# Attention logits from two fp32r parts on alternating row halves of the array, instead of three bf16 parts

## The chip, the cores and the metric

The kernel runs on one core of a Trainium2 chip. The metric is the device time of one execution in microseconds (us); lower is better.

## The reference

Two independent computations on inputs of 2048 x 576 each, joined along the last axis.

```python
# A: memory-augmented attention, 32 heads of 18, 4 segments of 512 rows
q,k,v = x@wq, x@wk, x@wv                 # split into heads and segments
for s in range(4):
    logits = qs @ ks.T * 18**-0.5 + mask # mask: -1e9 above the diagonal
    p = softmax(logits)
    a_dot = p @ vs
    a_mem = (phi(qs) @ M) / (phi(qs) @ z + 1e-6)
    o = g*a_mem + (1-g)*a_dot            # g = sigmoid(beta) of the head
    M += phi(ks).T @ vs;  z += phi(ks).sum(0)
out_a = concat(o) @ wo
# B: irfft2(rfft2(x) * (w_r + 1j*w_i))
```

Queries and keys come from weights scaled up by 200, so logits are large, and the kernel carries q and k in split precision.

## The kernel before

One program, in this order: forward FFT of B with the first weights of A (0 to about 73 us); projections of A beside the middle of the FFT on VectorE (to about 282 us); inverse FFT beside a prologue of attention (to about 356 us); attention with output projection (to the end). Instructions of each engine run in the order in which the code emits them.

**Projections.** `projections` runs over 4 segments g and 13 units each: nine `qk_unit`s (128 output rows of q and k by 512 columns, 14 fp32r matmuls in `passes`, L461) and four `v_unit`s. The matmuls of several units are in flight in five PSUM banks `pj`, while ScalarE (ACT) and VectorE (DVE) work off the older ones. A `qk_unit` splits its result into three bf16 parts in tile `sp3`: cast (L474), subtract in PSUM (L481), cast (L488), subtract again with a matmul against a negative identity `nid` (L490), cast (L491). SyncE's (SP) queue then writes them to DRAM: `qkD`, and for the two odd dimensions of each head (mt equal to 4) `reD`.

**Stacks.** Heads are worked on in groups n of eight (16 groups, four to a segment). `stack_dmas` reads a group's q or k back as a stack of 108 rows: dimension times part, in the combinations of parts that are needed (48+32+16 rows from `qkD`, 12 from `reD`). One matmul of 108 rows then gives the logits in split precision. Three buffers hold q stacks (`Qs`) and four k stacks (`Ks`). A quad k is half a group: four heads. Rows 108 and 109 hold the row maxima in two bf16 parts against -1 in `Ks`, so that the second pass subtracts them in the matmul.

**First pass, `s1(t)`,** for head t of 128: logits with queries on the partitions, in three PSUM tiles of the three banks `s1`: query blocks 2 and 0 in `pa` (384 and 128 columns, each with a matmul `idb` x `tri` of 128 columns that adds the causal mask, L666), block 3 in `pc` (512), block 1 in `pb` (256). DVE takes the row maxima: one reduction over blocks of 128 for `pa` (L667), one custom mask-and-reduce each for `pc` and `pb` (L661). `mpath(k)` turns a quad's maxima: small DVE, ACT and GpSimd (POOL) operations, a transpose on TensorE (PE), a copy, and a DMA into rows 108 and 109 of `Qs`.

**Second pass, `s2(t)`:** logits with keys on the partitions (L702: 512 columns, L706 and L707: 384 and 128 into one bank, L711: 256), exponentials on ACT (L703, L708, L712), and at a quad's end causal zeroing on POOL (L716). `pv` multiplies with the values in fp32, one 32-column tile of the array for each head of the quad (L731), in two of every four iterations.

**The loop** in `attention` runs t from 0 to 132. Iteration t emits, piece by piece in turn, s1 of head t+11 (generator `a`) and s2 of head t (generator `b`), then `pv` of the quad before; `run_bg` puts in a step of background work (`den`, `mixed`, `oproj`: L785, L804, L810, L851, L874). Up to t=116 both passes run in an iteration. `prologue` does s1 of the first 11 heads beside the inverse FFT, one piece at a time. `last_proj` and what stands around it form the end.

Of the kernel before, what the change touches and what calls it, by code (L numbers as in the profile page):

```python
# [340 lines left out]
BF=mybir.dt.bfloat16  # L341
# [43 lines left out]
class ATT:  # L385
    def __init__(s,nc,tc,io,cp,dp):
        s.nc,s.tc,s.io=nc,tc,io
        s.ident=cp.tile([128,128],F32,name="ident"); s.bm=cp.tile([126,7,19],F32,name="bm")
        s.tri=cp.tile([128,128],BF,name="tri"); s.idb=cp.tile([128,128],BF,name="idb")
# [3 lines left out]
        s.qkD=[d(f"qkD{i}",[8,3,128,512],BF) for i in range(4)]  # L393
        s.reD=[d(f"reD{i}",[24,32,512],BF) for i in range(4)]
# [68 lines left out]
    def qk_unit(s,g,mt,tp,pp):  # L463
# [5 lines left out]
        sp3=tp.tile([128,3,512],BF,name="sp3",bufs=3)  # L469
# [3 lines left out]
        j=[2,1,0] if mt>4 else [0,1,2]  # L473
        nc.scalar.copy(sp3[:,j[0]],ps)  # L474
# [6 lines left out]
        nc.vector.tensor_tensor(ps,ps,sp3[:,j[0]],op=OP.subtract)  # L481
# [6 lines left out]
        nc.scalar.copy(sp3[:,j[1]],ps)  # L488
        yield
        nc.tensor.matmul(ps,s.nid,sp3[:,j[1]],start=False,stop=True,skip_group_check=True)  # L490
        nc.scalar.copy(sp3[:,j[2]],ps)  # L491
        if mt!=4: nc.sync.dma_start(s.qkD[g][mt-(mt>4)].rearrange("i p c -> p i c"),sp3)
        else:
            for r,i,c,n in ((0,0,1,3),(0,1,1,2),(0,2,1,1),(64,0,3,3),(64,0,2,2),(64,0,1,1)):
                m={3:0,2:3,1:5}[n]; a=s.reD[g][r*12//64+2*m]
                x=sp3[r:r+64,i:i+c] if c==n else sp3[r:r+64,i:i+1].to_broadcast([64,n,512])
                nc.sync.dma_start(bass.AP(tensor=a.tensor,offset=a.offset,ap=[[512,64],[64*512,n],[1,512]]),x)
# [48 lines left out]
    def projections(s,xp,tp,pp,wv,pace,hook):  # L546

        live=[]
        s.nid=wv.tile([128,128],BF,name="nid"); s.nc.scalar.activation(s.nid,s.ident,AF.Copy,scale=-1.0)
# [25 lines left out]
    def att_setup(s,cp):  # L575
        nc,io=s.nc,s.io
        s.Qs+=[cp.tile([128,8,512],BF,name=f"Qs{i}") for i in range(1,3)]
        s.Ks+=[cp.tile([128,8,512],BF,name=f"Ks{i}") for i in range(1,4)]
# [10 lines left out]
    def stacks0(s,pool):  # L589

        t=pool.tile([128,9,512],F32,name="x0",tag="x0",bufs=1)
        q,k=[t[:,4*i:4*i+4].rearrange("p a c -> p (a c)").bitcast(BF).rearrange("p (a c) -> p a c",a=8) for i in range(2)]
        s.Qs,s.Ks,s.mask=[q],[k],t[:,8]; s.loaded=set()
        s.nc.sync.dma_start(s.mask,s.io["mask"])
        return s.stack_dmas(0,0)+s.stack_dmas(0,1)
    def masks(s):
        nc=s.nc
        nc.scalar.copy(s.tri,s.mask[:,384:])
        nc.scalar.copy(s.idb,s.ident)
# [553 lines left out]
```

## Time and profile before

| | us |
|---|---|
| runs (3) | 709.8, 709.96, 713.46; median 709.96 |
| the profiled execution | 710.93 |
| its span, first to last instruction | 709.2 |
| TensorE busy | 679.2 (96%) |
| VectorE busy | 551.2 (78%) |
| ScalarE busy | 451.3 (64%) |
| mean granted clock of TensorE | 1.000 |

PE is TensorE's matmuls, PEld its weight loads, which overlap them. A matmul's recorded duration includes a tail that overlaps the next one, so sums of durations say more than the time that passes; the distance from one start to the next is what a matmul costs. "f32" in a matmul row stands for fp32 and fp32r alike. A form such as 108*128 gives the rows and columns of the array in use.

### The profile page before, as it was taken

The page shows a single profiled execution, that of the slowest core. Times are in us where ns is not written, and L with a number is a line of the kernel's source. Part 1 is how long each engine was busy: PE and PEld are TensorE (multiplying, and loading weights), DVE is VectorE, ACT ScalarE, POOL GpSimd, SP SyncE. Part 2 cuts the span into 40 slices and gives each one's busy share as a digit, 9 for nine tenths or more (in the row PEclk, how much of TensorE's full clock was granted, in tenths as well). Part 3 has the DMA queues.
Part 4 walks back from the last instruction along what each step waited for, and adds up shares of the span by engine and source line. Part 5 has one row for each costly group of instructions (what it writes and reads, how often), then busy time and mean ns, then how long its engine had stood idle before and what let it go on. Part 6 is the DMA issues. An engine that isn't in the chain of part 4 may idle for free. (4 is left out here: it accounts for less than half of the span.)

```text
span 709.2 us, 14404 instructions
## 1 busy us (share of the span) xinstructions
PE 679.2 (96%) x4991; PEld 501.4 (71%) x4991; DVE 551.2 (78%) x1262; ACT 451.3 (64%) x986; POOL 209.8 (30%) x403
## 2 busy tenths in 40 slices
PE   4999999999999999999999899999999999999997
PEld 4988869879879879999954454445566445663487
DVE  5999979899799779787787887888657876567533
ACT  3665797485587474544378777777656776567421
POOL 5432000100200102655235333444323652235300
PEclk9999999999999999999999999999999999999999
DMA  8996455576385688899339886886656767442152
GB/s 308 289 286 171 132 159 185 162 208 203 91 234 177 167 209 294 199 253 262 110 111 207 182 175 137 197 202 159 152 131 176 190 159 158 89 127 67 28 156 82
DMA packets 71146, 123.80 MB, mean 175 GB/s; under 512 B 12184, under 2 KB 39174, under 8 KB 67482
## 3 DMA queue, kind: packets, MB, share of 16 engines
q1 hardware_dynamic: 64422, 106.89, 57.3%
q0 software_dynamic: 5632, 15.76, 8.2%
q8 instruction: 39, 0.64, 0.4%
q10 hardware_dynamic: 1020, 0.25, 0.2%
q14 instruction: 33, 0.27, 0.2%
HBM read 82.10 MB, written 39.81 MB: 172 GB/s over the span
## 5 line engine op out<-in xcount | busy, mean ns | idle before, releaser
L661 DVE CUSTOM_DVE_ANT_0 junk<-s,x 128x512 bf16<-128x512 f32 x248 | 137.0, 552 | 57.9 <-PE s L653 53.1
L716 POOL TENSOR_SCALAR_AFFINE_SELECT P<-P 128x512 f32<-128x512 f32 (+2 forms) x132 | 78.4, 625 | 113.6 <-ACT P L703 104.8
L667 DVE TENSOR_REDUCE mx<-s 128x4 f32<-128x512 f32 x128 | 87.7, 685 | 5.2 <-PE s L666 3.3
L703 ACT ACTIVATE P<-s 128x512 f32<-128x512 f32 x128 | 77.7, 607 | 12.6 <-PE s L702 4.6
L731 PE MATMUL pv<-P,vs 128*32 128x512 f32 (+3 forms) x1024 | 82.5, 439 | 0.1
L708 ACT ACTIVATE P<-s 128x512 f32<-128x512 f32 x128 | 77.5, 606 | 2.4 <-PE s L707 2.2
L712 ACT ACTIVATE P<-s 128x256 f32<-128x256 f32 x128 | 49.9, 390 | 44.7 <-PE s L711 44.2
L653 PE MATMUL s<-Ks,Qs 108*128 108x384 bf16 (+3 forms) x256 | 69.1, 301 | 1.5 <-DVE mx L667 1.2
L731 PEld LDWEIGHTS pv<-P,vs 128*32 128x32 f32 x1024 | 26.9, 109 | 45.3 <-issue 34.5
L461 PE MATMUL pj<-x,wqkh 128*128 128x512 f32 x162 | 56.5, 409 | 0.0
L653 PEld LDWEIGHTS <-Qs 108*128 108x128 bf16 x320 | 31.5, 98 | 24.4 <-issue 13.0
L205 DVE TENSOR_TENSOR Z<-t,t 128x290 f32<-128x290 f32 (+1 forms) x96 | 48.4, 555 | 0.1
L519 POOL MEMSET vt<- 128x32 f32 x16 | 2.4, 167 | 149.0 <-PE pm L529 127.7
L205 DVE TENSOR_TENSOR t<-Z 128x580 f32<-128x580 f32 x64 | 46.1, 757 | 0.0
L142 PE MATMUL f<-ftab,eh 128*128 128x290 f32 (+1 forms) x160 | 32.6, 323 | 11.8 <-DMA ftab<-ftab 9.2
L666 PE MATMUL s<-tri,idb 128*128 128x128 bf16 x256 | 43.0, 219 | 0.0
L295 PE MATMUL i<-civ,Y 128*128 128x256 f32 (+1 forms) x288 | 39.3, 289 | 0.2 <-POOL Y L280 0.2
L295 PEld LDWEIGHTS i<-civ,Y 128*128 128x128 f32 (+1 forms) x288 | 36.6, 181 | 1.0 <-POOL Y L280 0.4
L306 PE MATMUL i<-itab,T 128*128 128x290 f32 (+1 forms) x224 | 36.7, 306 | 0.0
L142 PEld LDWEIGHTS f<-ftab,eh 128*128 128x128 f32 (+1 forms) x160 | 26.1, 206 | 14.0 <-issue 8.6
L461 PE MATMUL pj<-x,wqkl 128*128 128x512 f32 x90 | 35.5, 395 | 0.0
L461 PE MATMUL pj<-xh,wqkl 128*128 128x512 f32 x90 | 35.5, 395 | 0.0
(210 smaller groups left out, 1830.2 us busy)
## 6 DMA issues: line engine op xcount, KB each, us to landing
qkD<-sp SPq DMA_DIRECT2D x32, 384.0 KB
xin<-xb SPq DMA_DIRECT2D x16, 384.0 KB
cfw<-cfw POOLq DMA_DIRECT2D x16, 384.0 KB, 4.3
civ<-civ POOLq DMA_DIRECT2D x16, 384.0 KB, 8.8
vs<-vD SPq DMA_DIRECT2D x16, 330.0 KB
vD<-vt SPq DMA_DIRECT2D x16, 311.0 KB
W<-w SPq DMA_DIRECT2D x16, 290.0 KB
yb<-yout SPq DMA_DIRECT2D x16, 290.0 KB
```

The costliest lines, as they stand in the source:

```text
L142: nc.tensor.matmul(p[:,r,:FP],x,t,start=n==0,stop=n==6)
L205: v.tensor_tensor(o,a,b,op=op)
L295: nc.tensor.matmul(p[:m,k],Y[i][:,q,c*128:c*128+m],cc[:,hl,o:o+256],start=n==0,stop=n==5)
L461: s.nc.tensor.matmul(out,a,b,start=i==0,stop=i==len(L)-1)
L653: nc.tensor.matmul(out,Q[:108,h,128*i:128*i+128],K[:108,h,:128*(i+1)],start=True,stop=True)
L661: nc.vector.tensor_tensor_reduce(out=junk[:,:w],in0=src,in1=s.mask[:,512-w:],scale=1.0,scalar=-3.0e38, op0=OP.add,op1=OP.max,accum_out=s.m ...
L667: nc.vector.tensor_reduce(out=s.mx[k][:,hh],in_=pa.rearrange("p (b c) -> p b c",c=128),axis=mybir.AxisListType.X,op=OP.max)
L703: nc.scalar.activation(P[0][:,hh],p0,AF.Exp,scale=SC)
L708: nc.scalar.activation(P[1][:,hh],p1,AF.Exp,scale=SC)
L712: nc.scalar.activation(P[2][:,hh],p2,AF.Exp,scale=SC)
L716: nc.gpsimd.affine_select(out=x[:,r],in_=x[:,r],pattern=[[0,r.stop-r.start],[1,128]],compare_op=OP.is_ge,fill=0.0,base=0,channel_multiplie ...
L731: nc.tensor.matmul(s.pvt[32*hh:32*hh+32,128*j:],vt[:,j,19*h:19*h+32],mv[0][:,hh,mv[1]],start=j==0,stop=j>1,skip_group_check=True)
```

## The change

- `qk_unit` keeps two fp32r parts, high and low, in a tile `sp` of two buffers: one cast on ACT and one subtraction on DVE that writes the low part to SBUF. The second and third cast, the matmul with `nid` and `nid` itself are gone. `qkD` and `reD` hold fp32.
- The stack of a quad has 54 rows (32+16 from `qkD`, 6 from `reD`) and two rows for the maxima, 56 in all. The first quad of a group stands on partitions 0 to 55, the second on 64 to 119. `quad_dmas(k)` loads one quad's q and k with six DMAs; both `Qs` and `Ks` have three buffers.
- s1 runs 12 heads ahead of s2, three quads, so s1 and s2 of an iteration stand on opposite row halves.
- s1 emits blocks 1 (256 columns), 3 (512), 2 (384), 0 (128) and then one mask matmul of 256 columns for the two blocks in `pa` together (`tri` is doubled). s2 emits 256, 512, 384 and 128 columns. The loop alternates them, so pieces of equal width follow each other.
- The transpose of `mpath` goes to the banks `s2` in attention; the maxima's rows are fp32; the -1 rows come from an SBUF tile `neg`.
- The prologue does 12 heads, each head's s1 in one go.

```diff
@@ qk_unit
-        sp3=tp.tile([128,3,512],BF,name="sp3",bufs=3)
+        sp=tp.tile([128,2,512],F32R,name="sp",bufs=2)
...
-        j=[2,1,0] if mt>4 else [0,1,2]
-        nc.scalar.copy(sp3[:,j[0]],ps)
+        hi,lo=(1,0) if mt>4 else (0,1)
+        nc.scalar.copy(sp[:,hi],ps)
...
-        nc.vector.tensor_tensor(ps,ps,sp3[:,j[0]],op=OP.subtract)
+        nc.vector.tensor_tensor(sp[:,lo],ps,sp[:,hi].bitcast(F32),op=OP.subtract)
...
-        nc.scalar.copy(sp3[:,j[1]],ps)
-        yield
-        nc.tensor.matmul(ps,s.nid,sp3[:,j[1]],start=False,stop=True,skip_group_check=True)
-        nc.scalar.copy(sp3[:,j[2]],ps)
@@ quad_dmas, in place of stack_dmas
+        nc=s.nc; n,b=divmod(k,2); g,G=divmod(n,4)
+        L=[]
+        for qk in range(2):
+            T=(s.Qs,s.Ks)[qk][n%3].bitcast(F32).rearrange("p a c -> p (a c)"); D=s.qkD[g][G+4*qk].rearrange("i (d b j) c -> b (i d) (j c)",b=2,j=4)[b]; o=64*b
+            L.append(lambda T=T,D=D,o=o: nc.sync.dma_start(T[o+16:o+48],D))
+            L.append(lambda T=T,D=D,o=o,qk=qk: nc.sync.dma_start(T[o:o+16],D[16*qk:16*qk+16]))
+            L.append(lambda T=T,o=o,qk=qk: nc.sync.dma_start(T[o+48:o+54],s.reD[g][6*qk:6*qk+6,8*G+4*b:8*G+4*b+4].rearrange("r h c -> r (h c)")))
...
@@ s1
+        Q,K=[x[n%3][64*qd:64*qd+54,hh] for x in (s.Qs,s.Ks)]; tp=s.sm
...
+        pb=s.ps1.tile([128,256],F32,name="s1",tag="s1")
+        mm(pb,1); red(pb,1)
         yield
         pc=s.ps1.tile([128,512],F32,name="s1",tag="s1")
         mm(pc,3); red(pc,3)
         yield
-        pb=s.ps1.tile([128,256],F32,name="s1",tag="s1")
-        mm(pb,1); red(pb,1)
+        pa=s.ps1.tile([128,512],F32,name="s1",tag="s1")
+        mm(pa[:,:384],2)
+        yield
+        mm(pa[:,384:],0,False)
+        yield
+        nc.tensor.matmul(pa[:,256:],s.idb,s.tri,start=False,stop=True,skip_group_check=True)
+        nc.vector.tensor_reduce(out=s.mx[k][:,hh],in_=pa.rearrange("p (b c) -> p b c",c=128),axis=mybir.AxisListType.X,op=OP.max)
         yield
@@ s2
+        Q,K=[x[n%3][64*qd:64*qd+56,hh] for x in (s.Qs,s.Ks)]; tp=s.tp
...
+        p2=s.ps.tile([128,256],F32,name="s2",tag="s2")
+        nc.tensor.matmul(p2,kk(2),q(256),start=True,stop=True)
+        nc.scalar.activation(P[2][:,hh],p2,AF.Exp,scale=SC)
+        yield
         p0=s.ps.tile([128,512],F32,name="s2",tag="s2")
...
         nc.tensor.matmul(p1[:,:384],kk(1),q(128),start=True,stop=True)
+        yield
         nc.tensor.matmul(p1[:,384:],kk(3),q(384),start=True,stop=True)
@@ attention
-            a=s.s1(t+11) if t+11<128 else iter(())
+            a=s.s1(t+12) if t+12<128 else iter(())
...
-            steps(a,1)
-            steps(b,1)
-            run_bg(0)
-            steps(a,1)
-            steps(b,1)
+            for _ in range(4):
+                steps(a,1)
+                steps(b,1)
+            steps(a,1)
+            steps(b,1)
+            if hh==1 and m is not None: steps(m,2); m=None
             if 4<=t-1<132: s.pv((t-5)//4,(t-5)%4)
             run_bg(1.2)
-            steps(a,1)
-            if hh==1 and m is not None: steps(m,1)
-            steps(b,1)
-            if hh==1 and m is not None: steps(m,1)
-            if hh==0 and k+2<32: m=s.mpath(k+2); next(m)
+            run_bg(0)
+            if hh==3 and k+3<32: m=s.mpath(k+3); next(m)
```

119 lines of the change are left out of this document (52 added, 67 removed).

## The prediction

> **What bounds the kernel now.** I read the page's busy times first, then its slices, its chain, the busy times by stage, and the timeline of TensorE inside one head. The page's first part and two of its slices:
>
> ```profile
> PE 679.2 (96%) x4991; PEld 501.4 (71%) x4991; DVE 551.2 (78%) x1262; ACT 451.3 (64%) x986; POOL 209.8 (30%) x403
> PE   4999999999999999999999899999999999999997
> DVE  5999979899799779787787887888657876567533
> ```
>
> TensorE (PE) is busy nearly everywhere; VectorE (DVE) is second and falls off in the right half, which is attention. The chain that ended last agrees: over a third of the span is PE work, and its costliest lines are attention's.
>
> ```profile
> PE 36%; DMA 3%; DVE 3%; ACT 2%; POOL 2%; issue 2%; ACTq 0%; SPq 0%; DVEq 0%; POOLq 0%
> PE pv L731 9%; PE s L653 8%; PE po L874 5%; PE s L702 3%; PE s L706 2%; PE pn L804 2%; PE po L903 2%; PE s L711 2%; PE s L666 2%; DMA rD<-U 1%; POOL P L716 1%; PE pd L785 1%; PE s L707 1%; DMA ux<-uD 1%; DVE junk L661 1%
> ```
>
> Busy times by stage: the projections of queries and keys, the inverse FFT with the prologue's heads, the 28 quads of attention in which a maxima head and an exponentials head run together, and from a second answer two single quads, a light one and one with output projection:
>
> ```profile
> core 0: us, PE busy (x) PEld busy (x) DVE busy (x) ACT busy (x) POOL busy (x), PEclk, DMA share, GB/s
> 81.59:261.06 179.47, 177.43 (x998) 149.21 (x998) 155.51 (x290) 124.42 (x244) 10.62 (x50) 1.00 0.62 181
> 320.00:356.17 36.17, 36.13 (x284) 33.83 (x283) 25.73 (x67) 14.48 (x35) 13.34 (x20) 1.00 0.73 185
> 363.25:641.51 278.26, 271.26 (x2339) 150.82 (x2339) 208.84 (x620) 200.94 (x482) 112.97 (x209) 1.00 0.69 157
> ```
> ```profile
> 413.89:421.67 7.78, 7.78 (x76) 4.07 (x74) 6.81 (x22) 6.16 (x16) 2.81 (x7) 1.00 0.62 152
> 531.34:543.92 12.58, 12.58 (x111) 8.82 (x109) 8.65 (x25) 8.35 (x23) 4.63 (x12) 1.00 0.58 163
> ```
>
> In all of them PE leaves gaps of 3% at most, at the full granted clock (1.00). In the light quad DVE has 1.0 us in 7.8 to spare, ACT 1.6; in the heavy one about 4. So PE time is worth its full price in heavy quads, and at most 1.0 us a quad in light ones.
>
> What a head costs PE (start, duration, engine, line; starts count, since matmuls overlap in their tails):
>
> ```profile
> 562.20 0.41 PE L810 MATMUL pb<-rd,sel 96*72 96x512 bf16 x1
> 562.45 0.27 PE L653 MATMUL s<-x 108*128 108x256 bf16 x1
> 562.56 0.27 PE L711 MATMUL s<-Qs,Ks 110*128 110x256 bf16 x1
> 562.67 0.33 PE L653 MATMUL s<-x 108*128 108x384 bf16 x1
> 562.84 0.22 PE L666 MATMUL s<-tri,idb 128*128 128x128 bf16 x1
> 562.89 0.22 PE L653 MATMUL s<-x 108*128 108x128 bf16 x1
> 562.95 0.22 PE L666 MATMUL s<-tri,idb 128*128 128x128 bf16 x1
> 563.01 0.38 PE L702 MATMUL s<-Qs,Ks 110*128 110x512 bf16 x1
> 563.23 0.38 PE L653 MATMUL s<-x 108*128 108x512 bf16 x1
> 563.45 0.33 PE L706 MATMUL s<-Qs,Ks 110*128 110x384 bf16 x1
> 563.61 0.22 PE L707 MATMUL s<-Qs,Ks 110*128 110x128 bf16 x1
> 563.67 0.38 PE L851 MATMUL pb<-rr,sel 96*126 96x512 bf16 x1
> 563.89 0.27 PE L653 MATMUL s<-x 108*128 108x256 bf16 x1
> ```
>
> From one 256-column start to the next is 1.44 us; without the 0.22 of L851 a head costs 1.22. A bf16 matmul takes 0.22 for 512 columns, 0.11 for 256, 0.165 for 384 and 0.055 for 128, and never waits for its weights. Of the 1.22, s1 has 0.66 (masks 0.11 of it) and s2 0.55.
>
> **Projections.** The third bf16 part goes: one matmul with `nid` and two casts in each of 36 units.
>
> ```profile
> L488 ACT CAST sp<-pj 128x512 bf16<-128x512 f32 x36 | 21.1, 588 | 18.5 <-DVE pj L481 18.5
> L491 ACT CAST sp<-pj 128x512 bf16<-128x512 f32 x36 | 20.8, 577 | 8.9 <-PE pj L490 8.4
> L490 PE MATMUL pj<-sp,nid 128*128 128x512 bf16 x36 | 13.9, 387 | 2.0 <-ACT sp L488 1.9
> ```
>
> PE is the bound here, so 36 x 0.22 = 7.9 us fall out. DVE then has 155.5 of 171.6 us, still under the span, so I take **-7**. The casts (36 x 1.165 = 42 us of ACT) are hidden already: nothing. The write of `sp` grows from 384 to 512 KB and has two buffers in place of three; the stage's 180 us hold 52 units (36 of these, 16 of values), one every 3.5 us, and PE has five banks ahead of it, so I take nothing. If that cover goes, at half a us of waiting a unit, it costs at most what was gained. The added SP issues in attention (12 where 8 were, each pair of quads) move the same bytes, for quads due eight heads later: nothing.
>
> **What the array will charge for halves.** No row here has two matmuls on the two row halves. The nearest are the one place with a 64-row matmul, its loads, the fp32 loads of L529, and attention's switch to 32-column tiles:
>
> ```profile
> 150.16 0.40 PE L461 MATMUL pj<-xh,wqkh 128*128 128x512 f32 x1
> 150.40 0.39 PE L490 MATMUL pj<-sp,nid 128*128 128x512 bf16 x1
> 150.72 0.46 PE L504 MATMUL ptr<-ident,ex 64*128 64x64 f32 x4
> 151.11 0.50 PE L461 MATMUL pj<-xl,wqkh 128*128 128x512 f32 x1
> 151.45 0.39 PE L461 MATMUL pj<-xh,wqkl 128*128 128x512 f32 x1
> ```
> ```profile
> 150.72 0.33 PEld L504 LDWEIGHTS ptr<-ident,ex 64*128 64x128 f32 x4 [0.23 <-issue]
> ...
> 230.03 1.19 PEld L529 LDWEIGHTS pm<-vt,pk 128*126 128x126 f32 x10
> ...
> 565.31 0.22 PE L707 MATMUL s<-Qs,Ks 110*128 110x128 bf16 x1
> 565.46 1.28 PE L731 MATMUL pv<-P,vs 128*32 128x512 f32 x16
> ```
>
> L461 is fp32r: 512 columns take 0.23 from start to start, 0.45 ns a column, so by proportion 256 take 0.116, 384 0.174, 128 0.058. Before L504 0.32 pass where the 512 bf16 columns need 0.22: entering the 64-row form costs 0.10. L504's four take 0.39 to the next start; its loads are (0.33-0.14)/3 = 0.06 apart, so 0.25 is work, 0.05 its first load and 0.09 leaving. The L461 behind it takes 0.34 instead of 0.23: its load, usually hidden, shows with 0.11. L707 to L731 takes 0.15 instead of 0.055: again 0.09 to 0.10. A bf16 load shows less: the L653 at 562.45 came 0.25 behind L810, a 512-column matmul that follows pv, so 0.03 over. So a switch costs 0.10, and 0.03 more into bf16 weights or 0.11 into fp32 ones. The Trainium skill, TensorEngine Tiling, Key Properties, says that changing the tiling mode drains the engine; these rows agree, with 0.09 to 0.10 us.
>
> A 128-column load takes 0.06 (L504, on 64 rows) to 0.11 (L529: (1.19-0.19)/9). L504's are transposes, so I take 0.11. The Trainium skill, TensorE: Matmul & The Clock Gate, LDWEIGHTS, has columns over 1.2, 107 ns, whatever the rows: L529 agrees, L504's 64-row loads came faster.
>
> Do two halves run at once? The nearest row is for column tiles:
>
> ```profile
> L731 PE MATMUL pv<-P,vs 128*32 128x512 f32 x224 | 29.8, 605 | 0.0
> ```
>
> 224 x 0.605 = 135 us of matmul lie in 29.8 us, over fourfold: the four column tiles run together, and load together. I take the same for row halves. Bounds for the four pairs (256, 512, 384, 128 columns): together 0.116+0.231+0.174+0.058 = 0.58, one after the other 1.16. The Trainium skill, TensorE: Matmul & The Clock Gate, Part 3, has a speedup of 3.07 for four row tiles; no run here shows it.
>
> **Attention, head by head.** The loop order after the change is maxima piece, exponentials piece, four times with equal widths on opposite halves, then one mask matmul of 256 columns on the full array (0.11, two of L666). Entering it costs 0.10+0.03, returning 0.10+0.11: 0.34. Heads with pv behind (jj 0 and 2, half of them) paid a switch in and out already; they add 0.13 and 0.08: 0.21. Mean 0.275. New head: 0.58+0.11+0.275 = 0.965 against 1.22, -0.255; by 116 heads (t=0 to 115) **-30**. Where background work (L851, L874) follows pv, the return from it is a new switch, +0.13; at most 58 heads, not all with a matmul: **+6**. Light quads get 1.0 from this and have 1.0 of DVE slack, which queues can't use up: I charge a third of it in half of the 28 quads, **+4**.
>
> Prologue: a head there has no partner: 0.58+0.11+0.21+0.13 = 1.03 against 0.66, +0.37 for 11 heads, 4.1, and a twelfth for 1.03, less 0.66 in attention: **+4.5**. The last 12 heads lack s1: 0.58 against 0.55, and 0.08 on six returns: **+1**. The m row comes three heads earlier relative to its use than now; nothing waits for it. Maxima and exponentials keep their instructions (the three DVE and three ACT ones of a head): nothing.
>
> Sum: -7-30+6+4+4.5+1 = **-21.5**. The profiled execution took 710.93 us (span 709.2, 1.7 around it), so 689.4; the runs' median, 709.96, is 1 lower: **689**, range of this case 676 to 702.
>
> **Rivals.**
> *Halves take turns* (slower). Then a head costs 1.16+0.11+0.275 = 1.545, +0.325, by 116 is +38, without the DVE charge: -7+38+6+4.5+1 = +42, **752**. For it: no row shows row halves together, and it is the only term that the switches, shown in rows, would leave alone. Against it: L731. It decides where four pairs cost over 0.795 us: the other terms give +4.5, so a head must come under 1.18, 0.385 of which is mask and switches. Less than a 63% overlap of the pairs loses.
>
> *Loads take turns.* Streams overlap, but eight loads of 0.11 share one path: a head is 0.88+0.11 and 0.23 of switches (fp32 loads counted already), or 0.13 where pv follows: mean 1.17, by 116 -6. Sum -7-6+6+4.5+1 = -1.5: **708**. For it: L529's ten loads follow each other at just that distance. Against it: pv's four loads don't add up. By the LDWEIGHTS rule of the Trainium skill named above, at 0.107 a load, it would be about 3 us less.
>
> *VectorE and ScalarE become the bound.* Each piece of s1 needs one of three banks that DVE frees. Now DVE waits 54.2 us for L653 in the row below; if such waits stay in spite of a quicker PE, because PE's order ties each s2 piece to the s1 piece ahead of it, the light half of the quads (14 x 1.0) gains nothing: -7-16+6+4.5+1 = -11.5, **698**.
>
> ```profile
> L661 DVE CUSTOM_DVE_ANT_0 junk<-s,x 128x256 bf16<-128x256 f32 x112 | 47.4, 424 | 54.2 <-PE s L653 49.7
> ```
>
> For it: DVE is 6.8 of 7.8 in light quads. Against it: the order puts maxima first.
>
> **How the numbers follow.** Halves together 0.52, DVE bound 0.14, loads in turn 0.10, halves in turn 0.24. I call 0.5% (3.5 us) about what a measurement of this kernel can tell from no change. Faster by more: 0.52+0.14 and 0.02 of the loads' case: 0.68. Within: 0.06 of that case. Slower: 0.24 and its other 0.02: 0.26. The range must reach into the slow case: up to 742 some 0.17 is left out above (752, with some 10 either way and a partial overlap below it), and at 668 about 0.03 below (switches partly hidden).
>
> **What would show it.** Right: in the timeline of a head, the s1 and s2 matmuls of a pair start within some tens of ns, the next pair a stream later; about 0.1 us before the mask and behind it; L490 gone; DVE's idle before L661 much smaller than 54; the 28 quads near 258 us. Wrong: a pair's second matmul starts a whole stream after its first (halves in turn, the 28 quads near 322 us), or PEld rows follow each other without gap 0.11 apart (loads), or DVE is busy over 95% in light quads.

## The result and the profile after

The changed kernel takes **755.63 us** (median of 4 runs, 754.22 to 758.32) against 710.4 us of the kernel before in the same comparison: ratio **1.063 (1.059 to 1.068)**, slower. Forecast were 689 us and at most 742; the sign was wrong too. In the table of experiments below, two of the four runs of one kernel, e3, took over 1.5% longer than its fastest and are left out of its time. The profiled execution's span is 756.6 us; its page, first and second part:

```profile
PE 694.3 (92%) x4827; PEld 509.5 (67%) x4827; DVE 558.3 (74%) x1263; ACT 414.5 (55%) x914; POOL 210.7 (28%) x405
PE   5999999999799967999998899898899989999997
DVE  5999888898698749688667677886666877675543
PEclk9999999999999988999959899999999999998999
```

PE's busy time rose from 679 to 694 us although it issues 164 matmuls fewer, and the granted clock is no longer full everywhere: its mean is 0.961, where it was 1.000.

```profile
core 0: 756.6 us, clock 0.961
```

The first casts of the projections and VectorE's custom maxima, each in one group over all its instructions, before and then after (columns: line, engine, operation, tiles, form, count; busy us, mean ns; idle us before them and who ended it):

```profile
L474 ACT CAST sp<-pj 128x512 bf16<-128x512 f32 x36 | 21.3, 591 | 12.1 <-PE pj L461 11.5 <-DMA reD<-sp 0.6
L661 DVE CUSTOM_DVE_ANT_0 junk<-s,x 128x512 bf16<-128x512 f32 x248 | 137.0, 552 | 57.9 <-PE s L653 53.1
```
```profile
L474 ACT CAST sp<-pj 128x512 fp32r<-128x512 f32 x36 | 21.1, 586 | 73.3 <-DMA qkD<-sp 38.4 <-PE pj L461 25.0 <-DMA reD<-sp 9.9
L658 DVE CUSTOM_DVE_ANT_0 junk<-s,mask 128x256 bf16<-128x256 f32 x248 | 137.6, 555 | 77.1 <-PE s L702 46.0
```

L488, L490 and L491 are gone, as they should be, but L474 now stands 48 us for transfers that read its own tile. VectorE's idle time before the custom maxima rose from 57.9 to 77.1 us, where the forecast named a fall as a sign of being right. By stages (us of the profiled executions, from the starts of the instructions named):

| | before | after |
|---|---|---|
| last matmul of the projections | 281.6 | 289.3 |
| exponentials product of 512 columns, t=0 | 356.2 | 376.1 |
| the same, t=4 | 363.25 | 385.09 |
| the same, t=116 | 641.51 | 684.70 |
| the same, t=127 | 663.4 | 710.9 |
| last projection of the output | 705.2 | 752.6 |

So 20 us are lost before attention starts, 2 in its first four heads, 21.3 in the 28 quads and 4 in the heads behind them. The 28 quads, with the columns of the busy times by stage:

```profile
385.09:684.70 299.61, 274.69 (x2229) 147.92 (x2227) 213.70 (x622) 200.87 (x483) 111.85 (x210) 0.95 0.65 151
```

299.6 us where 278.3 were and 258 were forecast; PE busy in 92% of it instead of 97%, at 0.95 of the clock.

Inside a head the change does what it says (TensorE's timeline; start, duration):

```profile
559.62 0.38 PE L650 MATMUL s<-Ks,Qs 54*128 54x256 f32 x1
559.62 0.38 PE L702 MATMUL s<-Qs,Ks 56*128 56x256 f32 x1
559.84 0.39 PE L650 MATMUL s<-Ks,Qs 54*128 54x512 f32 x1
559.85 0.39 PE L706 MATMUL s<-Qs,Ks 56*128 56x512 f32 x1
560.07 0.33 PE L650 MATMUL s<-Ks,Qs 54*128 54x384 f32 x1
560.08 0.33 PE L710 MATMUL s<-Qs,Ks 56*128 56x384 f32 x1
560.25 0.22 PE L650 MATMUL s<-Ks,Qs 54*128 54x128 f32 x1
560.25 0.22 PE L712 MATMUL s<-Qs,Ks 56*128 56x128 f32 x1
560.40 0.28 PE L671 MATMUL s<-tri,idb 128*128 128x256 bf16 x1
560.61 1.28 PE L732 MATMUL pv<-P,vs 128*32 128x384 f32 x16
561.83 0.40 PE L875 MATMUL po<-wol,oh 126*128 126x288 f32 x1
```

The two matmuls of a pair start 0 to 10 ns apart here, and in attention 411 of the 464 pairs start within 20 ns: the halves run together. From the pair of 384 columns to that of 128 pass 0.18 us, less than two loads of 0.11 one after the other. From the first pair to P times V pass 0.99 us, where 0.58 + 0.11 + a switch of 0.10 to 0.23 and a first load were reckoned with. The rival with the halves in turn, and the one with loads in turn, are out. The loss is elsewhere.

### The profile page after: what moved, and what is told of

Read it like the earlier page. It is cut to its first block, busy times and chain, and to the rows that moved or that the text cites. A ratio compares the mean times of both kernels' runs of the same rounds, so it can differ in the third digit from the quotient of the medians.

```text
span 756.6 us, 14166 instructions
## 1 busy us (share of the span) xinstructions
PE 694.3 (92%) x4827; PEld 509.5 (67%) x4827; DVE 558.3 (74%) x1263; ACT 414.5 (55%) x914; POOL 210.7 (28%) x405
## 5 line engine op out<-in xcount | busy, mean ns | idle before, releaser
L658 DVE CUSTOM_DVE_ANT_0 junk<-s,mask 128x256 bf16<-128x256 f32 x248 | 137.6, 555 | 77.1 <-PE s L702 46.0
L650 PE MATMUL s<-Ks,Qs 54*128 54x256 f32 (+1 forms) x320 | 88.3, 371 | 7.4 <-DVE mg L658 5.6
L732 PE MATMUL pv<-P,vs 128*32 128x512 f32 (+3 forms) x1024 | 89.7, 472 | 0.0
L650 PEld LDWEIGHTS s<-Ks,Qs 54*128 54x128 f32 x320 | 52.8, 196 | 44.5 <-DVE mg L658 15.6
L474 ACT CAST sp<-pj 128x512 fp32r<-128x512 f32 x36 | 21.1, 586 | 73.3 <-DMA qkD<-sp 38.4
L650 PE MATMUL s<-x 54*128 54x256 f32 x192 | 50.4, 360 | 4.8 <-DVE mg L658 3.5
L650 PEld LDWEIGHTS s<-x 54*128 54x128 f32 x192 | 30.6, 190 | 29.9 <-DVE mg L658 10.1
L295 PEld LDWEIGHTS i<-civ,Y 128*128 128x128 f32 (+1 forms) x288 | 37.3, 190 | 5.8 <-issue 3.7
L671 PE MATMUL s<-tri,idb 128*128 128x256 bf16 x128 | 37.3, 292 | 0.0
```

What stands on the lines that cost most here:

```text
L295: nc.tensor.matmul(p[:m,k],Y[i][:,q,c*128:c*128+m],cc[:,hl,o:o+256],start=n==0,stop=n==5)
L650: nc.tensor.matmul(out,Q[:,128*i:128*i+128],K[:,:128*(i+1)],start=first,stop=True,skip_group_check=not first)
L658: nc.vector.tensor_tensor_reduce(out=junk[:,:w],in0=src,in1=s.mask[:,512-w:],scale=1.0,scalar=-3.0e38, op0=OP.add,op1=OP.max,accum_out=s.m ...
L671: nc.tensor.matmul(pa[:,256:],s.idb,s.tri,start=False,stop=True,skip_group_check=True)
L732: nc.tensor.matmul(s.pvt[32*hh:32*hh+32,128*j:],vt[:,j,19*h:19*h+32],mv[0][:,hh,mv[1]],start=j==0,stop=j>1,skip_group_check=True)
```

## The experiments

Seventeen kernels ran, in groups that each have their own runs of the kernel before (medians 710.4 to 711.8). All but two are built on the changed kernel. "28 quads" is t=4 to 116, and behind it stands how much of it the granted clock was at half, both from one profiled execution. That is the slowest of the four for the change (758.3 us) and the fastest for e1 and e6 (729.8 and 716.2).

| run | us, median (lowest to highest) | ratio to before | 28 quads, us (half clock) |
|---|---|---|---|
| before | 710.4 (709.8 to 713.5) | | 278.3 (0) |
| after | 755.6 (754.2 to 758.3) | 1.063 (1.059 to 1.068) | 299.6 (28.9) |
| e1 three split buffers | 731.1 (729.8 to 731.8) | 1.028 (1.024 to 1.031) | 298.9 (26.8) |
| e2 next pair ahead | 765.8 (762.6 to 772.1) | 1.077 (1.071 to 1.084) | 314.9 (45.8) |
| e3 a fourth maxima bank | 839.4 (834.8 to 843.9) | 1.179 (1.170 to 1.188) | 362.8 (89.4) |
| e4 added products | 755.1 (754.2 to 760.4) | 1.063 (1.058 to 1.067) | 300.5 (23.9) |
| e5 = e1, P times V inside a head | 753.3 (747.4 to 755.7) | 1.059 (1.054 to 1.063) | 314.3 (37.3) |
| e6 = e1, m row on SP's queue | 720.3 (716.2 to 726.2) | 1.014 (1.008 to 1.021) | 286.9 (12.6) |
| e7 = e1, less maxima work | 726.5 (723.0 to 731.3) | 1.025 (1.019 to 1.030) | 292.3 (29.8) |
| e8 = before, less maxima work | 711.0 (709.0 to 713.2) | 1.000 (0.999 to 1.001) | 278.1 (0) |
| e9 = e6, P times V spread | 732.8 (728.9 to 735.1) | 1.027 (1.020 to 1.035) | 287.4 (23.4) |
| e10 = before, P times V spread | 715.9 (714.2 to 720.4) | 1.006 (1.004 to 1.009) | 283.1 (0) |
| e11 = e9, prologue in portions | 752.9 (749.5 to 753.9) | 1.055 (1.049 to 1.062) | 295.5 (42.9) |
| e12 = e9, products by zeros | 722.2 (721.8 to 724.3) | 1.016 (1.013 to 1.019) | 290.2 (10.2) |
| e13 = e9, more of them | 739.4 (737.8 to 744.3) | 1.040 (1.036 to 1.045) | 305.7 (6.8) |
| e14 = e6, products by zeros | 723.2 (720.2 to 726.7) | 1.017 (1.012 to 1.022) | 290.5 (3.4) |
| e15 = e6, mended in places | 718.0 (715.2 to 722.9) | 1.009 (1.006 to 1.012) | 287.3 (17.1) |
| e16 = e15 without the products | 723.3 (720.6 to 727.0) | 1.017 (1.013 to 1.020) | 290.5 (31.3) |
| e17 = e15, second try | 719.8 (716.6 to 721.9) | 1.012 (1.010 to 1.015) | 287.4 (13.7) |

### The write of the split parts (e1)

```diff
-        sp=tp.tile([128,2,512],F32R,name="sp",bufs=2)
+        sp=tp.tile([128,2,512],F32R,name="sp",bufs=3)
```
with one buffer less for W (3 to 2) and for the FFT's temporaries (8 to 7), to make room.

> The changed kernel with three buffers of the two-part tile in place of two (room for it comes from one buffer less of the FFT's weights and of its temporaries). Theory A, the write of 512 KB lands 3 to 10 us after its issue and with two buffers the next casts wait for it (48 us of ACT waits in the changed kernel's trace): the waits for that write fall below 15 us, the last matmul of the projections comes at 276 to 281 us instead of 289, the inverse FFT starts without its two idle stretches, and the time falls by 10 to 18 us, to 738 to 746. Rival B, PE's own work and VectorE's FFT work set the pace of the stage, the waits only fill ACT's spare time: the time falls by less than 4 us.

731.1 us: **24.5 us of the loss** come from the two buffers alone, more than the 10 to 18 expected. The waits of ScalarE (engine line waited for: us in total, times, longest), after and then in this run, both from 73 to 290 us:

```profile
ACT sp L474 <- DMA qkD<-sp: 38.4, 14, 7.0
```
```profile
ACT sp L474 <- DMA qkD<-sp: 7.1, 4, 2.5
```

The last projection's matmul starts at 271.1 instead of 289.3, which is 10.5 us earlier than before the change; forecast were 7. Attention doesn't gain from it: 298.9 us. From t=0 to 127 this run takes 330.4 us, before took 307.2.

### First tries at the attention: e2, e3, e4

In e1's 28 quads TensorE and VectorE wait for each other, TensorE for a maxima bank, VectorE mostly for pairs behind P times V (the waits of e1's 28 quads, TensorE's and VectorE's rows; before they were 0.8 and 53.1 us):

```profile
PE s L650 <- DVE mg L658: 9.8, 26, 0.7
DVE junk L658 <- PE s L702: 45.0, 39, 2.7
```

Three kernels, built on the changed one, test the order, the banks and the clock as the cause. e2 issues the next head's first pair ahead of this head's mask and P times V:

```diff
-            for _ in range(4):
+            for _ in range(3):
                 steps(a,1)
                 steps(b,1)
...
+            a1=s.s1(t+13) if t+13<128 else iter(())
+            steps(a1,1)
+            if hh<3:
+                b1=s.s2(t+1) if t+1<128 else iter(())
+                steps(b1,1)
+            steps(a,2)
+            steps(b,2)
```

> The changed kernel with the first pair of the next head emitted ahead of this head's mask matmul and pv, so that VectorE has a maxima piece to work on while TensorE does pv. Theory A, in light quads TensorE and VectorE stop each other in turn (TensorE for a bank, VectorE during pv): a light quad falls from 8.6 to 9.0 us to under 8.2, the 28 quads from 300 us to 280 to 290, the time to 735 to 748. Rival B, the half clock alone makes attention slow: quads at full clock stay at 8.6 us and the time changes by under 4 us.

It is 10 us slower than the changed kernel, with half clock in 46 us of the quads instead of 29; neither forecast of the time came, and the order alone doesn't help. e3 gives the maxima a fourth bank, taken from the exponentials' three:

```diff
-ps=es.enter_context(PP(tc,"ps",dict(s2=3,pv=1,post=1)))
+ps=es.enter_context(PP(tc,"ps",dict(s2=2,pv=1,post=1,sx=1)))
...
-        pb=s.ps1.tile([128,256],F32,name="s1",tag="s1")
+        pb=(s.ps.tile([128,256],F32,name="s1",tag="sx") if s.att else s.ps1.tile([128,256],F32,name="s1",tag="s1"))
```

> The changed kernel with four PSUM banks for the maxima pass in attention (the 256-column piece has its own) and two in place of three for the exponentials. Theory A, TensorE waits for a maxima bank and then VectorE for TensorE: with one more bank light quads fall to about 8 us and the 28 quads by 8 to 20 us. Rival B, the exponentials' banks are as tight: with two of them TensorE waits for ScalarE instead, and the quads get no shorter or longer by up to 10 us.

839.4 us, the slowest of all, and far beyond what either theory allowed. TensorE's wait went over to the exponentials (waits, 380 to 788 us):

```profile
PE s L710 <- ACT P L703: 29.0, 49, 4.9
```

So with two banks the exponentials hold TensorE up, as the maxima do with three. How much of the 63 us more in the 28 quads is the banks' doing isn't told apart here, since 89 us of them ran at half clock. e4 adds two products of 256 columns, which nobody reads, to each head up to t=33:

```diff
+            if t<34:
+                w=s.post("warm")
+                for i in range(2): nc.tensor.matmul(w[:,256*i:256*i+256],s.idb,s.tri,start=True,stop=True)
```

> The changed kernel with two more matmuls of 256 columns on the full array behind the mask matmul of each head up to t=33; nothing reads what they write. They add 0.22 us of TensorE work a head, 7.5 us in all, and raise the share of array cells at work. Theory A, the clock gate follows the share of the array's cells at work in stretches of 3.4 us, with a threshold near 0.4: no stretch at half clock between 376 and 457 us (27 us of them before), and in spite of the added work the first 32 heads get faster, from 81 us to 70 to 77. Rival B, the gate follows instructions or busy time, or half clock there is not what costs: the stretches stay or the 32 heads take 81 us or more.

755.1 us, no different from the change. The first 32 heads, after and in e4 (busy times; the clock is the third column from the end):

```profile
376.10:457.00 80.90, 73.47 (x526) 37.31 (x527) 56.17 (x163) 52.95 (x126) 26.95 (x49) 0.83 0.75 160
```
```profile
376.00:457.60 81.60, 74.22 (x590) 38.22 (x591) 56.31 (x163) 52.70 (x126) 27.13 (x49) 0.92 0.78 159
```

More work for the array, and the clock is granted at 0.92 instead of 0.83; the time is the same within 1%, not the 70 to 77 us of the first theory. That the added work costs 34 x 0.21 = 7 us of the array and shows 0.7 fits a clock that pays for it, and fits just as well TensorE having that time to spare; this run alone doesn't tell.

### The m row, P times V inside a head, and VectorE's share: e5 to e8

All but e8 stand on e1. In e1 ScalarE's queue stops at one place (its timeline: engine instructions, and ACTq for a transfer's issue):

```profile
403.40 0.60 ACT L713 ACTIVATE P<-s 128x512 f32<-128x512 f32 x1
411.44 0.62 ACTq L692 DMA_DIRECT2D x<-mts  x1
412.11 0.38 ACT L703 ACTIVATE P<-s 128x256 f32<-128x256 f32 x1 [8.11 <-DMA Qs<-qkD]
```

The issue of the m row, 16 KB, waits 7.4 us until a load of Q, issued on SP's queue at 402.60, has landed, and the exponentials behind it wait with it. The trace shows what holds it: the issue waits for semaphore 107, the counter on which its own transfer will report, and that Q load was the last to use it. In each of e1's three stands of over 1 us, and in each of the change's, the issue waited for its own semaphore in this way. So it is the program's reuse of a semaphore, not the data, that ties the two transfers together. Over the attention such stands come to 1.9 us before the change, 10.9 after, 13.1 in e1. e6 issues it on SP:

```diff
-        else: s.later(2,lambda: nc.scalar.dma_start(out,mt))
+        else: s.later(2,lambda: nc.sync.dma_start(out,mt))
```

> Three split buffers, and the transfer that writes the two rows of the maxima is issued on SP's queue, not on ScalarE's. With three split buffers alone ScalarE's queue stands still for 13.1 us in all at that issue, behind another transfer's completion. Theory that these waits are on the path: 28 quads fall from 298.9 by 6 to 13 us, the whole to 718 to 726 us. Theory that the banks' coupling sets the pace and the waits lie in its slack: the whole within 3 us of 731, or the waits turn up at SP and delay the loads of the next quads, with the same result or a worse one.

720.3 us: **10.7 us less than e1**. The first theory holds: these waits were on the path. e5 instead moves P times V (and the output's pieces) behind a head's second pair:

```diff
-            for _ in range(4):
+            for i in range(4):
                 steps(a,1)
                 steps(b,1)
+                if i==1:
+                    if 4<=t-1<132: s.pv((t-5)//4,(t-5)%4)
+                    run_bg(1.2)
```

> Three split buffers, and P times V and the output's pieces stand after a head's second pair instead of after its last. In the run with three split buffers alone TensorE and VectorE stop each other in turn: TensorE waits for a maxima bank, then VectorE waits for TensorE through P times V. Theory of coupling in turn: with two maxima pieces queued at VectorE when P times V begins, VectorE works through it, a quad without output falls from 8.6 to 9.0 us to under 8.3, and the 28 quads t=4 to 116 from 298.9 to 280 to 290 us, the whole to 712 to 722 us. Theory that the row switches and the fine order of two streams cost by themselves: one more switch pair per head, the quads at 8.8 to 9.4 us, the whole at 731 to 745 us.

753.3 us, light quads at 9.0 us: the rival's side, and worse than it said. VectorE's stand only changed its name (e5, 352 to 675 us):

```profile
DVE mx L672 <- PE s L671: 73.9, 73, 2.8
```

e7 reduces the 512-column maxima piece over its last 256 columns alone, which leaves half of that maximum out; e8 does so in the kernel before:

```diff
+            if i==3: src,w=src[:,256:],256
             junk=tp.tile([128,512],BF,name="junk",bufs=1)
```

> Three split buffers, and the 512-column maxima piece is reduced over its last 256 columns alone: half of that maximum is left out, so VectorE works some 0.25 us less per head. Theory that VectorE's release of the maxima banks sets the pace after the change: the 128 heads lose 15 to 35 us, the whole comes to 696 to 716 us. Theory that TensorE (streams and row switches) sets it: under 6 us, 725 to 731 us.

> The kernel before with the same cut: its 512-column maxima piece is reduced over its last 256 columns alone. Theory that TensorE's streams bound the attention before the change: under 8 us gained, 702 to 710 us. If VectorE had been as tight before as after, it gains as much as the changed kernel does from the cut, 15 to 35 us.

e8 gains nothing (711.0), as forecast. e7 gains 4.6 us, not 15 to 35, and its interval overlaps that of e1: VectorE's own work alone doesn't set the pace. A light quad at full clock goes from 8.62 to 8.08 us for 1.0 us less of VectorE, so half of the cut comes off:

```profile
420.53:428.61 8.08, 7.61 (x71) 3.80 (x71) 5.85 (x21) 5.59 (x14) 1.32 (x5) 1.00 0.78 188
```

TensorE is busy in 7.61 of it, VectorE in 5.85; neither fills it. VectorE's work thus counts where it delays a bank, but it isn't the bound by itself.

### The hand-off around P times V: e9 to e11

A light quad of e6, and VectorE and TensorE at its P times V:

```profile
404.79:413.41 8.62, 7.61 (x73) 3.81 (x72) 6.92 (x21) 6.42 (x16) 2.77 (x7) 1.00 0.67 157
```
```profile
405.12 0.42 DVE L658 CUSTOM_DVE_ANT_0 junk<-s,mask 128x256 bf16<-128x256 f32 x1 [0.49 <-PE s L702]
406.45 0.50 PE L650 MATMUL s<-Ks,Qs 54*128 54x512 f32 x1 [0.43 <-DVE mg L658]
```

The brackets hold the idle time before and who ended it. Behind each P times V, which lasts 1.2 us, VectorE has run out of pieces, since at most three banks can be full; a head later TensorE has run out of banks. TensorE's four stands in this quad (0.43, 0.11, 0.36 and 0.11 us) are the 1.0 us by which it exceeds TensorE's 7.61. e9 spreads P times V over three heads, each time behind the mask, where the array's form changes anyway:

```diff
-        for j in ((0,3),(),(1,2),())[jj]:
+        for j in ((0,),(3,1),(2,),())[jj]:
```

> Three split buffers, the m row on SP's queue, and the products of P times V spread over three heads of a quad (1024, 1024 and 512 columns' time of two passes, in place of two groups every second head). In the run before it, light quads take a steady 8.62 us at full clock with TensorE busy 7.6 and VectorE 6.9: VectorE stands 0.5 us in each group of P times V, having at most three banks of maxima queued, and TensorE stands 0.4 us before each such group. Theory that this hand-off over three banks sets the pace: the light quad comes to 7.6 to 8.1 us, the whole to 700 to 712 us. Theory that TensorE's own work sets it: 8.4 us or more a quad, the whole within 3 us of 720.

> The kernel before with the same spreading of P times V. Its light quads take 7.8 to 8.3 us, with TensorE busy in 7.8 to 8.0 of them, so nothing stands there that the spreading could remove: within 2 us of 710. If it gains as the changed kernel does, the spreading is a gain of its own that has nothing to do with the change.

Both halves of the answer surprised. A light quad at full clock falls to 7.61 us, on the spot that the theory named:

```profile
417.36:424.97 7.61, 7.60 (x72) 3.89 (x70) 6.49 (x21) 6.00 (x15) 2.24 (x6) 1.00 0.98 149
```

Quads 9 and 20 give 7.81 and 7.76 (e6: 8.67 and 8.63). These are the best; over the eight light quads that stay at full clock in both (5, 6, 7, 9, 10, 12, 20, 28), e9's are shorter by 0.62 us in the mean, from 1.01 shorter to 0.08 longer. But the whole is 12.5 us slower than e6. e10 loses 4.6 us, beyond the 2 that I allowed it, so the spreading is no gain by itself. Most of e9's loss is the clock's. The heads t=116 to 127 do the same work in both kernels but for the order of P times V; e6 and then e9:

```profile
644.70:668.00 23.30, 23.04 (x142) 11.12 (x142) 13.28 (x23) 16.33 (x39) 10.62 (x17) 1.00 0.24 66
```
```profile
647.90:688.30 40.40, 39.66 (x149) 16.62 (x149) 13.24 (x24) 18.29 (x39) 12.87 (x20) 0.54 0.13 38
```

23.3 us at full clock and 40.4 at 0.54: here half clock costs about 17 us.

e11 adds to e9 that a prologue head's five steps are issued in three portions:

```diff
-            for _ in s.s1(t): pass
+            x=s.s1(t)
             for j in range(3):
+                for _ in range((1,1,3)[j]): next(x,None)
                 if q: q.pop(0)()
                 yield
+            for _ in x: pass
```

> As the run with three split buffers, the m row on SP's queue and P times V spread, and in the prologue the maxima of a head are issued in three portions, each with its loads, in place of all five steps at once. The inverse stage took 3.4 us more than before (77.4 against 74.0). If TensorE's in-order queue, stopped at a maxima bank in the prologue, is the reason: 2 to 4 us off that stage and off the whole. If the reason is the work itself, within 1 us of the run without.

The opposite: the inverse stage takes 86.6 us instead of e9's 77.4 (first to last matmul of the inverse, 273.2 to 359.8), and half clock rises to 42.9 us in the quads. The idea that TensorE's in-order stop in the prologue costs the 3.4 us falls; why the portions cost 10 us stays open.

### The clock: e12 to e17

What the clock goes with can be read off the matmul records. I cut each run's attention (350 to 700 us) into the steps of 3.41 us in which the granted clock changes, and sum in each, over the matmuls, stream time at full clock times the share of rows (halves) and columns (quarters) that the matmul uses: the share of the array at work. An fp32 matmul stands twice in the records, and each of its records counts as two passes. The counts below shift by up to ten or so with the stream time taken for fp32r (0.43 to 0.45 ns a column); the picture stays. Over 19 profiled executions:

| share of the array at work in a step | at full clock: next step is at half | at half clock: next step is at full |
|---|---|---|
| under 0.36 | 46 of 48 | 0 of 51 |
| 0.36 to 0.40 | 28 of 35 | 11 of 37 |
| 0.40 to 0.44 | 14 of 44 | 63 of 65 |
| 0.44 and over | 4 of 1650 | 17 of 18 |

In the kernel before, the mean of this share in the first 32 heads is 0.83 and no step of its attention lies under 0.47; after the change it is 0.46, in e6 and e9 0.52. That TensorE is busy doesn't help: e9 has steps in which its records leave no gap, at half clock,

```profile
357.00:363.80 6.80, 6.80 (x30) 3.94 (x30) 5.04 (x13) 4.45 (x11) 2.76 (x6) 0.50 1.13 179
```

and from 650 to 684 us it stays there with TensorE's records over 33.6 of the 34 us (streams alone fill some 72 to 87% of each step) and 0.28 to 0.36 of the array at work. Nor does busy time tell which steps at half clock end: TensorE's records fill over 95% of 157 of these 171 steps, and 90 of the 157 were followed by full clock. The Trainium skill, TensorE: Matmul & The Clock Gate, section HAM oscillation, gives the rule that the clock stays up without idle gaps of TensorE over some 3.4 us. By that rule these heads would have run at full clock; the trace disagrees, and the share of the array fits it. A low share and waits of TensorE go together in these kernels, so that the table alone doesn't prove the share to be the cause; the kernels that add work to the array test it. No step at half clock has more than 0.46, and in e9 a stage with half-filled products, once down, stays down: the heads from t=116 on have exponentials without a partner. In e6 the same heads enter at full clock and keep it.

The last runs fill the array. e12 widens e9's mask product to all 512 columns with zeros, and adds products that nobody reads in t=0 to 5 and 115 to 127; e13 adds two more zero products per head to that, and e14 does e12's edit to e6 (`tri` has 256 columns of zeros ahead of the two masks):

```diff
-        nc.tensor.matmul(pa[:,256:],s.idb,s.tri,start=False,stop=True,skip_group_check=True)
+        nc.tensor.matmul(pa,s.idb,s.tri,start=False,stop=True,skip_group_check=True)
...
+            if t<6 or 115<=t<128:
+                w=s.post("warm")
+                for i in range(2): nc.tensor.matmul(w[:,256*i:256*i+256],s.idb,s.tri[:,256:],start=True,stop=True)
```
and in e13, ahead of the mask:
```diff
+        for i in range(2): nc.tensor.matmul(pa[:,256*i:256*i+256],s.idb,s.tri[:,:256],start=False,stop=True,skip_group_check=True)
```

> The spread version (three split buffers, m row on SP's queue, P times V over three heads), with the mask's product widened from 256 to 512 columns (the added ones are zeros, 0.11 us of the full array per head), and two products of 256 columns that nobody reads per head in t=0 to 5 and 115 to 127. Theory of the clock: half clock goes from 23.4 us in the 28 quads to under 10 and away from t=116 to 127, which falls from 40.4 to some 24 us; the quads keep 7.7 to 8.3 us where light; the whole comes to 702 to 716 us from 732.8. Theory that the clock is a symptom of TensorE's waiting and costs nothing by itself: 733 to 745 us.

> As the run with the widened mask, with two more products of 256 zero columns ahead of the mask in each head (0.32 us of the full array per head in all). Theory of the clock: no half clock left in the 28 quads, light quads at 8.0 to 8.6 us as TensorE's own work rises by 0.85 us a quad, the whole within 6 us of the run with the widened mask alone, on the better side if that still shows half clock. Theory that the clock costs nothing: 0.2 us a head more than that run, some 25 us.

> Three split buffers, m row on SP's queue, P times V in two groups as in the change, with the widened mask and the added products of t=0 to 5 and 115 to 127. Both theories of the light quad: it stays at 8.6 us or a little more, since VectorE's stand during P times V is still there. Theory of the clock: half clock falls from 12.6 us to near nothing in the 28 quads, and the whole comes to 712 to 718 us against 720.3; against the spread and filled version it is 5 to 12 us longer. If the clock costs nothing: 720 to 728 us.

e12 does more work than e9 and is **10.6 us faster** (722.2 against 732.8): the clock costs time by itself. t=116 to 127 come back to full clock:

```profile
651.50:678.20 26.70, 26.00 (x171) 11.83 (x171) 13.39 (x23) 17.19 (x39) 12.99 (x20) 1.00 0.19 57
```

But it reaches 722, not 702 to 716. The filling is paid wherever TensorE is the bound: quads 25 to 27 take 36.7 us in e12, 38.9 in e13, 35.7 in e9. e13 shows that end of it, 739 us with 6.8 us of half clock left: my 6 us between e12 and e13 were 17, the price of the added work, which removed only 3.4 us of half clock. In e14 the filling takes half clock from 12.6 to 3.4 us and gives all of it back, 723.2 us against 720.3, the same within the noise, with light quads at 8.8 instead of 8.6; forecast were 712 to 718.

e15 to e17 tried to take each remedy only where it bites. e15 is e6 with P times V spread for seven of the quads, the transpose of the maxima one head later, the widened mask in 14 heads and the added products for t under 6; e16 is that without the two kinds of products; e17 has the later transpose only before t=16 and the widened mask also in heads 24 to 35:

```diff
-        for j in ((0,3),(),(1,2),())[jj]:
+        for j in (((0,),(3,1),(2,),()) if k in (4,5,6,8,9,11,19) else ((0,3),(),(1,2),()))[jj]:
...
+        o=0 if t-12 in (0,1,2,3,4,5,12,13,14,15,44,45,46,47) else 256
-        nc.tensor.matmul(pa[:,256:],s.idb,s.tri,start=False,stop=True,skip_group_check=True)
+        nc.tensor.matmul(pa[:,o:],s.idb,s.tri[:,o:],start=False,stop=True,skip_group_check=True)
...
-            if hh==1 and m is not None: steps(m,2); m=None
+            if hh==2 and m is not None: steps(m,2); m=None
```

> Three split buffers, m row on SP's queue, P times V spread over three heads in seven light quads alone (k 4, 5, 6, 8, 9, 11, 19), the transpose of the maxima one head later so that it doesn't wait for POOL, and the array kept at work with products by zeros in heads 0 to 5, 12 to 15 and 44 to 47, where the runs before fell to half clock. If the two causes account for the loss: 28 quads at 272 to 280 us (278.3 before, 286.9 in the run with the m row on SP's queue), the whole at 702 to 712 us, so on a level with or below the kernel before. If something else holds it, it stays at 715 to 725 us.

> The same without the products by zeros. Theory that half clock in the first quads and at t=44 to 47 costs time: 3 to 6 us longer than the run with them, with 6 to 13 us of half clock in the 28 quads. If it costs nothing there: the same or up to 2 us shorter.

> As the mended version, but the transpose is one head later only before t=16, and the widened mask also stands in heads 24 to 35. In the mended version TensorE stood 4.34 us at 407 for the two rows of the maxima, and quads 7, 8 and 11 ran 3.4 us each at half clock. If hand-off and clock account for the loss: 28 quads fall from 287.3 to 275 to 281 us, the whole to 704 to 712 us. If the loss is elsewhere (row switches, the order of two streams): the whole stays at 714 to 719 us.

e15 comes to 718.0 us and is the fastest of the versions, still 0.9% (0.6 to 1.2) behind the kernel before. e16 is 5.2 us slower than e15 with 31 us of half clock against 17: once more the clock, within the forecast of 3 to 6. In e15 the m row came too late for quad 5:

```profile
407.07 0.55 PE L704 MATMUL s<-x 56*128 56x256 f32 x1 [4.34 <-DMA x<-mts]
```

e17 mends that place, and TensorE stands elsewhere, for another load, a quad later (waits, 358 to 648 us):

```profile
PE s L651 <- DMA Ks<-reD: 1.9, 1, 1.9
```

with half clock behind it. By e17's own expectation, 719.8 us speaks against hand-off and clock as the whole account: in the first 32 heads, once TensorE is quicker, loads come late too, and in both of these stands the array's share fell to some 0.11 and 0.15, with half clock in the next step. No version that I ran beats the kernel before.

## Why the prediction was wrong, point by point

*Projections, -7.* The matmul with `nid` was worth what I gave it and a little more: 10.5 us with three buffers. The step that failed is the line behind it, "the write of `sp` ... I take nothing. If that cover goes, ... it costs at most what was gained". Two buffers of 512 KB, each held until its write has landed, cost 24.5 us, over three times the 7 us of the gain. The cover I named, five banks ahead, stops as soon as the cast that empties them waits.

*Halves together, switches.* Right. The head shown starts its pairs within 10 ns and stands close to where the sum put it. In five heavy quads its price holds too: 17, 19 and 25 to 27 took 63.0 us before and 58.8 in e6, -0.85 a quad for the -1.02 (4 x 0.255) less background switches that I had. But 16 and 18, as heavy and as full of TensorE's records before, took 0.5 and 1.0 us more in e6; no run tells why.

*Attention, -30 +6 +4.* This is the term that failed: -20 in the sum, +21 in the 28 quads after the change, +8.6 in e6, where the two DMA waits are gone. I multiplied TensorE's saving by 116 heads, with a charge of 4 us for VectorE. Set out by quads, e6 against before:

| quads | before | e6 | difference |
|---|---|---|---|
| 17, 19, 25, 26, 27: heavy, shorter in e6 | 63.0 | 58.8 | -4.2 |
| 2, 4 to 7, 9, 10, 12, 20, 28: light | 83.2 | 87.4 | +4.2 |
| 1, 3, 11: with half clock in e6 | 25.7 | 31.6 | +5.9 |
| the other ten, 16 and 18 among them | 106.4 | 109.1 | +2.8 |

A light quad should have come to 6.8 us by TensorE, and to something between that and 7.8 by my charge; it came to 8.62. I saw that VectorE had 1.0 us to spare and treated 6.8 as a floor that queues can't quite reach. The light quad that I showed was also one of the fullest: others, such as 4, 5 and 11, took 8.7 to 9.1 us before the change with TensorE busy in 8.0 or 8.1 of them, so TensorE's work wasn't the only limit there even then. What binds in e6 is the hand-off: a pair ties the two streams together, three banks a stream, and a P times V of 1.2 us between them, which is longer than the pieces in the banks last. e9 showed it by spreading P times V: 7.61 us at full clock in the best quad. Of the 1.8 us between 6.8 and 8.62 that is 1.0; no run shows what the other 0.8 are. e5, the other way to break it, made it worse, so the explanation holds for e9's order only.

*VectorE and ScalarE become the bound, 698.* The rival nearest to what happened in the light quads, at chance 0.14, and too mild: I let the light quads gain nothing, and they lost 0.4 us each. As worded it is wrong as well: VectorE's work by itself wasn't the bound (e7 took 1.0 us of it out of a light quad and got 0.5 back), the waits in turn were.

*The m row, "nothing waits for it".* Nothing waits for the row, but ScalarE's queue waits to issue it, for a semaphore that another transfer holds: 1.9 us before, 13.1 in e1, and moving the issue is worth 10.7 us. I had asked who needs the transfer, not who stands behind its issue.

*The clock.* No term, no rival. The profile of before showed 1.00 everywhere, and I took it as given. The change does away with half of the array's work by running two halves at once; the other engines hold the pace, the share falls to 0.5, and the clock halves in places. e12 against e9 and e16 against e15 show it at 5 to 11 us, t=116 to 127 of e9 at 17.

*Prologue, +4.5; last heads, +1.* The inverse stage took 77.4 us in e1 against 74.0 (+3.4), t=116 to 127 23.1 against 21.9 (+1.2). Both right.

From 755.6 us down to the forecast of 689: 24.5 are the split buffers (e1), 10.7 the m row's issue (e6), both shown by taking them away. Some 29 of the other 31 lie in e6's 28 quads (286.9 against 258, in its fastest run), between hand-off, clock and loads that then come late. How these divide isn't settled: each remedy brought out another of the three.

## What to carry to other kernels

A saving on the busiest engine is worth its price only in the stretches where that engine alone is the bound: go quad by quad, and where another engine has a tenth to spare, ask how many pieces lie between the two and what long work interrupts them, before any of it is counted. A transfer that grows, or an issue that is moved, is costed by what holds its buffer and by what stands behind its issue on the same queue, not by its consumer. A change that packs the array tighter can fall under the clock's line when others hold the pace, so the share of the array at work belongs in the sum.

## What the runs showed of the hardware that I had not expected

- In these runs the granted clock goes with the share of the array's rows and columns at work in a step of 3.41 us, not TensorE's busy time: under 0.36 it fell in 46 of 48 steps, from 0.44 on in 4 of 1650, and it returned at 0.40 and over in 80 of 83. e12 adds work to the array and is 10.6 us faster than e9. A stage that leaves half of the rows empty can't always climb back: 23.3 us of work took 40.4.
- A transfer's issue can stand on its engine's queue until an unrelated load from another queue has landed, when both report on the same semaphore: 7.4 us for a 16 KB write, with ScalarE's exponentials behind it.
- Two fp32r matmuls on the two row halves start 0 to 10 ns apart, and the change of the array's form costs 0.1 us: the 128-column pair ahead of the mask takes 0.15 us for 0.06 of stream, the mask ahead of P times V 0.21 for 0.11, as the forecast took it from other rows.
